# Gated linear recurrence and an ELU network on one core: unit 0 first, weights between its steps, other DMA queues, decays a round ahead

## The chip, the core and the metric

The kernel runs on one core of a Trainium2 chip. The core has a matrix engine (TensorE, PE), a vector engine (VectorE, DVE), an activation engine (ScalarE, ACT), a general engine (GpSimd, POOL) and an engine that only issues transfers (SyncE, SP). Each engine takes its own queue of instructions in order, and semaphores hold an instruction until what it reads is there. The metric is the time of one execution on the device in microseconds; lower is better.

## The reference

```python
def _attn_ref(q, k, v, a_re, a_im):          # B, H, S, D = 4, 8, 768, 48
    mag = np.sqrt(a_re * a_re + a_im * a_im)
    scale = np.minimum(mag, 0.999) / (mag + 1e-06)
    a_re_n, a_im_n = (a_re * scale, a_im * scale)
    for t in range(S):
        ar, ai = (a_re_n[:, :, t, :, None], a_im_n[:, :, t, :, None])
        new_re = ar * S_re - ai * S_im
        new_im = ar * S_im + ai * S_re
        kv = np.einsum('bhd,bhe->bhde', k[:, :, t], v[:, :, t])
        S_re, S_im = (new_re + kv, new_im)
        y[:, :, t] = np.einsum('bhd,bhde->bhe', q[:, :, t], S_re)

def _moe_ref(x, w_in, w_out):                # x: 3072 x 384, w_in: 384 x 2048, w_out: 2048 x 384
    h = x @ w_in
    g = np.where(h > 0.0, h, np.exp(np.minimum(h, 0.0)) - 1.0)
    return (g @ w_out).astype(np.float32)
```

The output y of the first part, heads side by side, is x of the second. The two weights come as float64 and the kernel rounds them to float32 itself, from their two 32-bit words.

## The kernel before

The 3072 tokens are cut into 12 units of 256: 128 positions of a pair of the four sequences. A unit goes through three groups of stages.

The decays (`squares`, `logarithms`, `angles`, `carried`) turn a_re and a_im into a logarithm l and an angle th. The gating (`turns`, `decays`, `waves`, `gated`) sums them along the positions on TensorE, takes exponentials E and F and cosines and sines cs, and multiplies them into q and k, which gives qg and kg. E's rows at the end of each 64 positions also go out to memory (`ends`) and come back transposed as T. The recurrence, for each of the two sequences n, transposes qg and kg (`transposed`), forms scores and masks them (`scores`, tile a), carries the state S over two blocks of 64 positions (`states`; S = (S + kv) * T on VectorE and GpSimd) and sums the output y (`values`). `seam` then copies y by DMA into x, in which 384 features lie over three groups of 128 partitions.

The network follows: `hidden` makes two of the 16 blocks of g (six products, then Relu and Exp on ScalarE and one fused step on VectorE), eight calls to a unit; `project` makes a quarter of the 16 products of one 128-token half, eight calls to a unit. The PSUM tiles of `hidden` and `project` share three buffers (tag mlp), those of the other products share three more (tag w).

The order is written out by hand. A step has 16 slots; in each slot stand the recurrence of unit step - 2, the gating of unit step - 1, the decays of unit step, one weight piece while there are any, and one call of `hidden` or `project` for unit step - 3 (lists CC, BB, A and M). So unit 0 crosses three steps before its first `hidden`, and the 28 weight pieces (12 of w_in, 512 columns, and 16 of w_out, 128 rows) stand one to a slot in the first 28 slots. `load_weights` loads a piece and rounds it with six steps on VectorE and one addition on GpSimd between them. All transfers but carry (the phase that one unit hands to the unit after next) are issued by SyncE.

Of the kernel before, what the change touches and what calls it, by code (L numbers as in the profile page):

```python
# [29 lines left out]
WC = 512  # L30
# [22 lines left out]
def _general(  # L53
# [291 lines left out]
    def seam(y_sb):  # L345
        x = sb.tile([C, NI, GT], FP32, tag="x", bufs=2, name="x")
        for h in range(H):
            e = 0
            while e < D:
                i, r = divmod(h * D + e, C)  # L350
                n = min(D - e, C - r)
                nc.sync.dma_start(
                    out=x[ds(r, n), i], in_=y_sb[ds(h % 2 * HP + e, n), h // 2]
                )
                e += n
        return x
# [81 lines left out]
def kernel(  # L438
# [87 lines left out]
    def load_weights(dst, src):  # L526
# [3 lines left out]
        if src.dtype == FP32:  # L530
            nc.sync.dma_start(out=dst, in_=src)
            return
        n = dst.shape[-1]
        w = sb.tile([C, n, 2], U32, tag="g", bufs=5, name="w64")
        nc.sync.dma_start(out=w.rearrange("p n two -> p (n two)"), in_=src)
        lo, hi = w[:, :, 0], w[:, :, 1]
        f = sb.tile([C, n], U32, tag="ee", bufs=4, name="wf")
        p = sb.tile([C, n], U32, tag="ee", bufs=4, name="wp")
        nc.vector.tensor_scalar(
# [3 lines left out]
        nc.vector.scalar_tensor_tensor(  # L543
            out=f, in0=hi, scalar=TOP, in1=p, op0=ALU.bitwise_and, op1=ALU.bitwise_or
        )
        nc.vector.tensor_scalar(
# [3 lines left out]
        nc.vector.scalar_tensor_tensor(  # L550
            out=p, in0=lo, scalar=2.0**-52, in1=p, op0=ALU.mult, op1=ALU.mult
        )
        nc.gpsimd.tensor_tensor(out=p, in0=p, in1=f, op=ALU.add)  # L553
        nc.vector.tensor_scalar(
            out=hi, in0=hi, scalar1=EXP, scalar2=None, op0=ALU.bitwise_and
        )
        nc.vector.scalar_tensor_tensor(
# [6 lines left out]

    def new(tag, bufs=1, shape=None):
        return sb.tile(shape or [C, NB, H, D], FP32, tag=tag, bufs=bufs, name=tag)

    def squares(u):
        x = nat[u]
        ar, ai = x["ar"], x["ai"]  # L570
        nc.vector.tensor_reduce(
# [6 lines left out]
        x["m2"], sq = new("m2"), new("e")  # L578
        nc.scalar.activation(out=x["m2"], in_=ar, func=AF.Square)
        nc.scalar.activation(out=sq, in_=ai, func=AF.Square)  # L580
        nc.gpsimd.tensor_tensor(out=x["m2"], in0=x["m2"], in1=sq, op=ALU.add)  # L581

    def logarithms(u):


        x = nat[u]
        ar, ai = x["ar"], x["ai"]
        lm, lr = x["m2"], new("lr")
        nc.scalar.activation(out=lm, in_=lm, func=AF.Ln)
        nc.scalar.activation(out=lr, in_=ar, func=AF.Ln)  # L590
        e, x0 = new("e"), new("x0")
        nc.scalar.activation(out=x0, in_=lr, func=AF.Exp, scale=-1.0)
        nc.scalar.activation(out=e, in_=lm, func=AF.Exp, scale=-0.5, bias=ln_eps)  # L593
        nc.gpsimd.tensor_tensor(out=lr, in0=ar, in1=x0, op=ALU.mult)
        nc.gpsimd.tensor_tensor(out=x0, in0=ai, in1=x0, op=ALU.mult)
        x["l"] = new("l")
        nc.vector.scalar_tensor_tensor(  # L597
            out=flat(x["l"]), in0=flat(lm), scalar=2 * float(np.log(CAP)), in1=flat(e),
            op0=ALU.min, op1=ALU.subtract,
        )  # L600
        nc.vector.scalar_tensor_tensor(
            out=flat(x0), in0=flat(lr), scalar=-2.0, in1=flat(x0), op0=ALU.add, op1=ALU.mult
        )
        x["t"] = x0
# [3 lines left out]
    def angles(u):  # L608
        x = nat[u]
        x["th"] = new("th")  # L610
# [12 lines left out]
    def turns(u):  # L623
        x = nat[u]
        x["z"] = new("z")
        for n in range(NB):
# [5 lines left out]
            r = new("rnd", 2, [C, HD])  # L632
# [11 lines left out]
    def decays(u):  # L644
        x = nat[u]
        x["E"], x["F"] = new("E"), new("F")
        x["T"] = new("T", 3, [2 * D, NB, C // L, H])
# [12 lines left out]
        nc.sync.dma_start(  # L660
# [3 lines left out]
        for i in range(2):  # L664
            for n in range(NB):
# [83 lines left out]
    def values(u, n):  # L749
# [17 lines left out]
        if n == 0:  # L767
            x["y"] = new("y", 1, [C, NP, GT])
# [167 lines left out]
```

## Time and profile before

| | us |
|---|---|
| median of three runs | 917.97 (916.97 to 921.32) |
| the profiled execution | 920.53 |
| its span, first to last instruction | 918.7 |
| TensorE busy in it | 716.1 |
| ScalarE, VectorE, GpSimd busy | 369.8, 301.9, 227.0 |

The profile's groups name a line, an engine, an operation, and the tile that is written and those that are read; behind them stand the busy time, the mean duration in ns, the idle time ahead of the group and what ended it. A matrix product in float32 is two instructions in these counts. Windows give, for a stretch of the span, its length and then the busy time of TensorE, its weight loads, VectorE, ScalarE and GpSimd, TensorE's granted clock (1.00 is full), the share of the DMA engines and GB/s.

### The profile page before, as it was taken

The numbers are of one execution on the slowest core, as the hardware profiler recorded it, in microseconds if no ns is written. First come the engines' busy times: TensorE is split into PE (matmuls) and PEld (weight loads), VectorE is DVE, ScalarE is ACT, GpSimd is POOL, SyncE is SP. The second block draws the span as 40 slices with busy tenths as digits, with TensorE's granted clock in tenths as the row PEclk, the third lists the DMA queues.
The fourth block names the chain that finished last, engine by engine and source line by source line (L and its number), as shares of the span: only waits on it lengthen the run. The fifth ranks groups of instructions, "written<-read, shape, count | busy, mean of one in ns | idle before, by whom it ended". The sixth has DMA issues, their size and how long they took to land.

```text
span 918.7 us, 13005 instructions
## 1 busy us (share of the span) xinstructions
PE 716.1 (78%) x5346; PEld 523.7 (57%) x5346; DVE 301.9 (33%) x454; ACT 369.8 (40%) x555; POOL 227.0 (25%) x159
## 2 busy tenths in 40 slices
PE   0100002749999999899999999999999999999997
PEld 0000002538667677576676676776766767778684
DVE  2777875314233232133142331331422312112020
ACT  2310302617437257165273381562733714433040
POOL 1322425222302312313233123132330230110000
PEclk9955556659999999999999999999999999999999
DMA  8243143230142212311411422124113021010100
GB/s 210 60 169 103 20 136 68 37 69 3 34 86 37 48 40 37 76 12 35 87 20 22 83 36 56 33 35 86 25 23 76 3 54 33 2 35 2 35 2 20
DMA packets 177485, 47.04 MB, mean 51 GB/s; under 512 B 165720, under 2 KB 173832, under 8 KB 177416
## 3 DMA queue, kind: packets, MB, share of 16 engines
q1 hardware_dynamic: 177096, 46.09, 24.7%
q8 instruction: 44, 0.72, 0.3%
q14 instruction: 25, 0.20, 0.1%
q0 software_dynamic: 320, 0.03, 0.0%
HBM read 36.55 MB, written 4.79 MB: 45 GB/s over the span
## 4 chain that ended last, share of the span: by engine, by line
PE 48%; POOL 14%; issue 12%; SPq 10%; DVE 10%; DMA 4%; ACT 1%; POOLq 0%; DVEq 0%
PE mlp L797 25%; PE mlp L813 12%; SPq L783 5%; POOL kg L689 4%; SPq L509 3%; POOL wp L553 3%; PE w L704 2%; PE w L712 2%; POOL F L686 2%; POOL E L686 2%; PE w L733 2%; DMA x<-y 2%; DVE wf L543 2%; DVE wp L550 2%; PE y L762 1%
## 5 line engine op out<-in xcount | busy, mean ns | idle before, releaser
L797 PE MATMUL mlp<-x,w_in 128*128 128x256 f32 x1152 | 277.9, 392 | 30.1 <-DMA x<-y 23.6
L797 PEld LDWEIGHTS mlp<-x,w_in 128*128 128x128 f32 x1152 | 218.3, 195 | 73.7 <-issue 18.7
L813 PE MATMUL mlp<-w_out,g 128*128 128x384 f32 x768 | 258.5, 490 | 0.0
L813 PEld LDWEIGHTS mlp<-w_out,g 128*128 128x128 f32 x768 | 143.2, 190 | 92.7
L804 DVE SCALAR_TENSOR_TENSOR g<-ee,mlp 128x512 f32<-128x512 f32 x96 | 64.3, 685 | 271.6 <-ACT ee L803 271.6
L802 ACT ACTIVATE ee<-mlp 128x512 f32<-128x512 f32 x96 | 56.9, 593 | 150.9 <-PE mlp L797 149.1
L704 PE MATMUL w<-ident,qg 128*96 128x128 f32 x192 | 27.2, 288 | 107.6 <-DVE qg L689 107.6
L745 POOL TENSOR_TENSOR S<-S,T 96x384 f32<-96x384 f32 x40 | 33.0, 825 | 273.2 <-DVE S L744 252.4
L819 ACT COPY o<-mlp 128x384 f32<-128x384 f32 x24 | 11.5, 479 | 213.8 <-PE mlp L813 213.8
L704 PEld LDWEIGHTS w<-ident,qg 128*96 128x96 f32 x192 | 21.9, 132 | 112.7 <-DVE qg L689 99.2
L581 POOL TENSOR_TENSOR m<-m,e 128x768 f32<-128x768 f32 x12 | 21.7, 1812 | 175.7 <-ACT e L580 175.7
L803 ACT ACTIVATE ee<-ee 128x512 f32<-128x512 f32 x96 | 60.5, 630 | 2.8
L553 POOL TENSOR_TENSOR wp<-wp,wf 128x384 f32<-128x384 f32 (+1 forms) x28 | 32.1, 1145 | 100.5 <-DVE wp L550 97.6
L628 PE MATMUL w<-th,sum_turns 128*128 128x384 f32 x48 | 19.6, 534 | 43.3 <-ACT th L611 43.3
L689 DVE TENSOR_TENSOR qg<-E,cs 128x1536 f32<-128x1536 f32 x12 | 21.1, 1758 | 93.0 <-POOL E L686 93.0
L733 PEld LDWEIGHTS w<-vn,kg 64*96 64x96 f32 x704 | 37.3, 172 | 17.7 <-issue 9.6
L733 PE MATMUL w<-vn,kg 64*96 64x48 f32 x704 | 40.5, 257 | 7.6 <-DVE z L636 7.6
L597 DVE SCALAR_TENSOR_TENSOR l<-m,e 128x768 f32<-128x768 f32 x12 | 23.6, 1968 | 66.1 <-ACT e L593 66.1
L705 ACT COPY qt<-w 96x512 f32<-96x512 f32 x48 | 25.8, 584 | 40.7 <-PE w L704 40.7
L689 POOL TENSOR_TENSOR kg<-F,cs 128x1536 f32<-128x1536 f32 x12 | 41.6, 3463 | 0.9
L744 DVE TENSOR_TENSOR S<-w,S 96x384 f32<-96x384 f32 x40 | 22.1, 552 | 51.1 <-PE w L733 35.6
L628 PEld LDWEIGHTS w<-th,sum_turns 128*128 128x128 f32 x48 | 9.9, 210 | 47.7 <-ACT th L611 43.3
(65 smaller groups left out, 730.8 us busy)
## 6 DMA issues: line engine op xcount, KB each, us to landing
w<-in_moe_w_in_dram SPq DMA_DIRECT2D x12, 512.0 KB
w<-in_moe_w_out_dram SPq DMA_DIRECT2D x16, 384.0 KB
ar<-in_a_re_dram SPq DMA_DIRECT2D x24, 192.0 KB
ai<-in_a_im_dram SPq DMA_DIRECT2D x24, 192.0 KB
q<-in_q_dram SPq DMA_DIRECT2D x24, 192.0 KB
k<-in_k_dram SPq DMA_DIRECT2D x24, 192.0 KB
vn<-in_v_dram SPq DMA_DIRECT2D x24, 192.0 KB
out_dram<-o SPq DMA_DIRECT2D x24, 192.0 KB
```

What stands on the lines that cost most here:

```text
L553: nc.gpsimd.tensor_tensor(out=p, in0=p, in1=f, op=ALU.add)
L686: nc.gpsimd.tensor_tensor(out=g, in0=x[key], in1=g, op=ALU.mult)
L689: eng.tensor_tensor(out=o, in0=g.rearrange("p n h d -> p (n h) d").unsqueeze(2).to_broadcast(shape), in1=x["cs"], op=ALU.mult,)
L704: nc.tensor.transpose(t[:, h], x[key + "g"][:, n, h0 + h], ident)
L733: nc.tensor.matmul(g[:, h], lhsT=x["kg"][ts(c, L), n, h], rhs=vn[u % 2][ts(c, L), n, h, 0:D], start=True, stop=True,)
L745: nc.gpsimd.tensor_tensor(out=new_s, in0=new_s, in1=wide, op=ALU.mult)
L783: nc.sync.dma_start(out=x[ds(r, n), i], in_=y[ds(h % 2 * HP + e, n), h // 2])
L797: nc.tensor.matmul(t[:, e], lhsT=w_in[:, i, ts(f + e, C)], rhs=x["x"][:, i], start=(i == 0), stop=(i == NI - 1),)
L802: nc.scalar.activation(out=e, in_=t, func=AF.Relu, scale=-1.0)
L803: nc.scalar.activation(out=e, in_=e, func=AF.Exp, scale=-1.0)
L804: nc.vector.scalar_tensor_tensor(out=x["g", f // 4][:, f % 4 : f % 4 + 2], in0=e, scalar=-1.0, in1=t, op0=ALU.add, op1=ALU.max)
L813: nc.tensor.matmul(x["o"], lhsT=x["g", f // 4][:, f % 4, ts(n, C)], rhs=w_out[:, f], start=(f == 0), stop=(f == NF - 1),)
```

## The change

**Order.** Unit 0 goes straight through all its stages before anything else, with steps of the weight rounding between them. Then come rounds of 16 slots. Round r holds `hidden` of unit r, the gating and the recurrence of unit r + 1, and `project` of units r - 1 and r - 2 (four calls each; of unit 0 all eight in round 1 and the next slot). Units 1 and 2 have their decays in the same round as their gating. From unit 3 on the decays stand a round ahead, in slots 8 to 12.

**Weights.** They are cut into 14 parts (6 of w_in, 1024 columns; 8 of w_out, 256 rows). A part's seven steps are all on VectorE and are handed out one by one: 22 in unit 0, 56 in round 0, the rest in the first slots of round 1. The rows of w_in are loaded in an order of their own: the 48 + 16 + 48 + 16 rows of each group of 128 partitions are chosen so that `values` can write three quarters of x straight from PSUM in place, and `seam` moves only 16-partition pieces, six instead of ten.

**Queues.** `seam` and T go by GpSimd's queue, `ends` by ScalarE's. T is two transfers of 48 x 32 single elements instead of four of half that size.

**Engines and buffers.** The products of `squares`, `logarithms` and the k side of `gated` are on VectorE for unit 0, and on GpSimd later; q's two products are on VectorE always. Most tiles of the decays and the gating share one tag with six buffers; kg, kt and o have one buffer instead of two.

On TensorE, at the start of the program, this stood before (qg, kg, qt and kt are the gated q and k and their transposes, vn is v, sum_turns and sum_logs are constant matrices):

```order
L628 MATMUL w<-th,sum_turns 128x384 x2
L650 MATMUL w<-l,sum_logs 128x384 x2
L704 MATMUL w<-ident,qg 96x128 x8
L704 MATMUL w<-ident,kg 96x128 x8
L628 MATMUL w<-th,sum_turns 128x384 x2
L712 MATMUL w<-qt,kt 64x64 x16
L733 MATMUL w<-vn_72,kg 96x48 x16
L650 MATMUL w<-l,sum_logs 128x384 x2
```

And this stands at the end of unit 0's recurrence now, with unit 1 behind it (the tag n holds th and l):

```order
L790 MATMUL y<-a,vn_72 64x64 x16
L797 MATMUL y<-qt,S 48x64 x8
L831 MATMUL mlp<-x,w_in 128x256 x24
L664 MATMUL w<-n,sum_turns 128x384 x2
L686 MATMUL w<-n,sum_logs 128x384 x2
L739 MATMUL w<-ident,qg 96x128 x8
L831 MATMUL mlp<-x,w_in 128x256 x6
```

The sums of the next unit, which stood among unit 0's products, now stand behind unit 0's first four `hidden` calls.

On VectorE, in round 0, the rows around unit 1's rounding are now these (L838 is g, L567 to L585 are the weight steps, L669 and L672 the rounding of the summed angle):

```order
L621 SCALAR_TENSOR_TENSOR n<-n 128x768
L626 SCALAR_TENSOR_TENSOR n<-n 128x768
L634 TENSOR_REDUCE least<-ar 128x1
L637 TENSOR_REDUCE most<-ai 128x1
L838 SCALAR_TENSOR_TENSOR g<-ee,mlp 128x512
L567 TENSOR_SCALAR wp<-w_427 128x1024
L571 SCALAR_TENSOR_TENSOR wf<-w_427,wp 128x1024
L574 TENSOR_SCALAR wp<-wf 128x1024
L838 SCALAR_TENSOR_TENSOR g<-ee,mlp 128x512
L578 SCALAR_TENSOR_TENSOR wp<-w_427,wp 128x1024
```

Before, a piece's steps stood together, and the decays and the rounding between whole pieces; now single steps alternate with the stages.

On VectorE, in a steady round, the rows from the second block's state on were these before:

```order
L744 TENSOR_TENSOR S_3459<-w,S_2610 96x384
L744 TENSOR_TENSOR S_3462<-w,S_3459 96x384
L597 SCALAR_TENSOR_TENSOR l<-m_3370,e 128x768
L601 SCALAR_TENSOR_TENSOR x_3486<-lr,x_3486 128x768
L804 SCALAR_TENSOR_TENSOR g<-ee,mlp 128x512 x4
L717 TENSOR_TENSOR a<-w,mask 128x512
```

and are these now:

```order
L779 TENSOR_TENSOR S<-w,S 96x384 x2
L621 SCALAR_TENSOR_TENSOR n<-n 128x768
L626 SCALAR_TENSOR_TENSOR n<-n 128x768
L634 TENSOR_REDUCE least<-ar 128x1
L637 TENSOR_REDUCE most<-ai 128x1
L838 SCALAR_TENSOR_TENSOR g<-ee,mlp 128x512 x3
L752 TENSOR_TENSOR a<-w,mask 128x512
```

The two fused steps of the decays have changed places, and the two reductions stand behind them, ahead of the last three g of the unit that is in `hidden`.

The core of the diff:

```diff
-        nc.gpsimd.tensor_tensor(out=p, in0=p, in1=f, op=ALU.add)
+        yield nc.vector.tensor_tensor(out=p, in0=p, in1=f, op=ALU.add)
...
+    def products(u):
+        return nc.vector if u == 0 else nc.gpsimd
...
-        nc.sync.dma_start(
+        nc.scalar.dma_start(
             out=ends.rearrange("n c h d -> c n (h d)"),
             in_=x["E"][L - 1 :: L].rearrange("p n h d -> p n (h d)"),
         )
-        for i in range(2):
-            for n in range(NB):
-                nc.sync.dma_start(
-                    out=x["T"][ts(i, D), n].rearrange("p c h -> p (c h)"),
-                    in_=ends[n].rearrange("c h d -> d (c h)"),
-                )
...
+        for i in range(2):
+            nc.gpsimd.dma_start(
+                out=x["T"][ts(i, D)].rearrange("p n c h -> p (n c h)"),
+                in_=x["ends"].rearrange("n c h d -> d (n c h)"),
+            )
...
+        for j in range(2):
+            for i in range(NI):
+                nc.gpsimd.dma_start(
+                    out=x["x"][ds(j * HP + D, G), i], in_=x["y"][ds(j * HP + i * G, G)]
                 )
...
+    once = recurrence(decaying(0, 1, 1, 3, 3) + gating(4, 5, 5, 6), 7)
+    steady = recurrence(gating(0, 1, 2, 3), 6)
+    early = decaying(8, 9, 9, 12, 12)
...
+    between = {angles: 3, decays: 4, gated: 4}
+    for at, fn in once:
+        fn(0)
+        if fn is gated:
+            load_qk(1)
+        converts(between.get(fn, int(at >= 7)))
+    load_v(1)
+    for at, fns in enumerate(plan):
+        if at < 2 * SLOTS:
+            fetches(1 if at < 8 else at % 2)
+            converts(3 if at < 8 else 4 if at < SLOTS else 3)
+        for fn in fns:
+            fn()
```

`recurrence(first, base)` lays the transposes, scores, states and values of the two sequences at slots base + 0 to base + 8 and `seam` at base + 9; `converts(n)` issues the next n steps of the weight rounding.

More of the change, by code (lines that the diff above doesn't have):

```diff
@@ new lines, with fetches, converts @@
+    parts = [("in", m) for m in range(NI * DF // WC)] + [("out", m) for m in range(NF // WF)]
+    ahead, steps = list(parts), []
+    def fetches(n):
+        for kind, m in ahead[:n]:
+            fetch(kind, m)
+        del ahead[:n]
+    def converts(n):
+        for _ in range(n):
+            while not steps or next(steps[0], None) is None:
+                del steps[:1]
+                if not parts:
+                    return
+                steps.append(rounded(*parts.pop(0)))
+    SLOTS = 16
@@ new lines, in recurrence @@
+    def recurrence(first, base, n_only=None):
+        at = [[0, 1, 2, 3, 5], [3, 4, 6, 7, 8]]
+        fns = [
+            [
+                lambda u, n=n: transposed(u, "q", n), lambda u, n=n: transposed(u, "k", n),
+                lambda u, n=n: scores(u, n), lambda u, n=n: states(u, n),
+                lambda u, n=n: values(u, n),
+            ]
+            for n in range(NB)
+        ]
+        plan = [(base + x, fn) for n in range(NB) for x, fn in zip(at[n], fns[n])]
+        return sorted(first + plan + [(base + 9, seam)], key=lambda x: x[0])
```

264 lines of the change are left out of this document (134 added, 130 removed).

## The prediction

> **What bounds the kernel now.** I read the page from the top, then cut the span where the first product of the second half, `hidden`, begins.
>
> ```profile
> span 918.7 us, 13005 instructions
> PE 716.1 (78%) x5346; PEld 523.7 (57%) x5346; DVE 301.9 (33%) x454; ACT 369.8 (40%) x555; POOL 227.0 (25%) x159
> PE   0100002749999999899999999999999999999997
> ```
> ```profile
> 0.00:197.30 197.30, 30.08 (x280) 22.43 (x280) 115.73 (x197) 47.46 (x59) 66.97 (x55) 0.66 0.41 98
> 197.30:324.70 127.40, 121.29 (x883) 87.77 (x883) 35.69 (x48) 60.55 (x92) 32.10 (x20) 0.95 0.25 44
> 324.70:758.60 433.90, 412.43 (x3193) 300.82 (x3193) 124.33 (x168) 212.18 (x322) 117.61 (x76) 0.98 0.25 44
> 758.60:912.30 153.70, 152.29 (x992) 112.66 (x992) 26.13 (x41) 49.19 (x82) 10.32 (x8) 1.00 0.08 18
> 912.30:918.70 6.40, 0.00 (x0) 0.00 (x0) 0.00 (x0) 0.46 (x1) 0.00 (x0) 0.84 0.10 36
> ```
>
> TensorE (first column after the length) is full from 197 us on and nearly idle before: of the 202.6 us it idles, 167 lie ahead of 197.3, 29 in the three rows between, 6.4 behind its last product. The view of waits says for whom it waits:
>
> ```profile
> PE w L704 <- DVE qg L689: 107.6, 2, 98.5
> PE w L628 <- ACT th L611: 43.3, 1, 43.3
> PE mlp L797 <- DMA x<-y: 23.6, 21, 3.1
> ACT z L676 <- DMA carry<-z: 1.3, 1, 1.3
> ```
>
> The first 147 us are VectorE's: it runs 28 weight conversions in a row while unit 0 waits between them for its step. In the steady part a unit waits once, for x to land. So there are two questions: when does a full TensorE begin, and what does each later round wait for? TensorE's products themselves are the same in both kernels.
>
> **The opening: what VectorE carries.**
>
> ```profile
> L539 DVE TENSOR_SCALAR wp<-w 128x512 uint32<-128x512 uint32 x12 | 5.0, 420 | 16.4 <-DMA w<-in_moe_w_in_dram 16.3
> L539 DVE TENSOR_SCALAR wp<-w 128x384 uint32<-128x384 uint32 x16 | 5.6, 352 | 2.2 <-DMA w<-in_moe_w_out_dram 2.1
> L543 DVE SCALAR_TENSOR_TENSOR wf<-w,wp 128x512 uint32<-128x512 uint32 x12 | 8.3, 693 | 0.4
> L543 DVE SCALAR_TENSOR_TENSOR wf<-w,wp 128x384 uint32<-128x384 uint32 x16 | 8.9, 559 | 0.6
> L553 POOL TENSOR_TENSOR wp<-wp,wf 128x512 f32<-128x512 f32 x12 | 16.0, 1333 | 54.2 <-DVE wp L550 54.2
> ```
>
> 128 columns more cost 0.068 us in the first kind and 0.134 in the second. Carried on (an estimate) a 1024-wide step takes 0.69 or 1.23 us, a 768-wide one 0.56 or 0.96. A part is three steps of the first kind, three of the second and the addition. The addition has no VectorE row at this width; I take the second kind (below it lies the first kind, above it POOL's 1.33 per 512). That is 7.0 us for each of 6 w_in parts and 5.5 for each of 8 w_out parts, 86 us in all. What matters is where they stand, since VectorE takes its queue in order. The other durations:
>
> ```profile
> 4.92 1.28 ACT L579 ACT_TABLE_LOAD   x1 [4.92 <-DMA ar<-in_a_re_dram]
> L589 ACT ACTIVATE m<-m 128x768 f32<-128x768 f32 x12 | 10.1, 843 | 58.9 <-POOL m L581 58.8
> L655 ACT ACTIVATE E<-w 128x384 f32<-128x384 f32 x24 | 11.8, 492 | 26.7 <-PE w L650 26.7
> L705 ACT COPY qt<-w 96x512 f32<-96x512 f32 x48 | 25.8, 584 | 40.7 <-PE w L704 40.7
> L594 POOL TENSOR_TENSOR lr<-ar,x 128x768 f32<-128x768 f32 x12 | 21.8, 1816 | 49.2 <-DMA T<-ends 36.7 <-ACT x L592 12.5
> L595 POOL TENSOR_TENSOR x<-ai,x 128x768 f32<-128x768 f32 x12 | 28.2, 2353 | 0.9
> L686 POOL TENSOR_TENSOR F<-k,F 128x768 f32<-128x768 f32 x12 | 21.6, 1803 | 0.0
> L689 POOL TENSOR_TENSOR kg<-F,cs 128x1536 f32<-128x1536 f32 x12 | 41.6, 3463 | 0.9
> L689 DVE TENSOR_TENSOR qg<-E,cs 128x1536 f32<-128x1536 f32 x12 | 21.1, 1758 | 93.0 <-POOL E L686 93.0
> L601 DVE SCALAR_TENSOR_TENSOR x<-lr,x 128x768 f32<-128x768 f32 x12 | 11.5, 956 | 17.1 <-POOL x L595 17.1
> L571 DVE TENSOR_REDUCE least<-ar 128x1 f32<-128x768 f32 x12 | 11.3, 944 | 0.0
> L636 DVE TENSOR_TENSOR z<-w,rnd 128x384 f32<-128x384 f32 x24 | 13.4, 557 | 0.8
> L804 DVE SCALAR_TENSOR_TENSOR g<-ee,mlp 128x512 f32<-128x512 f32 x96 | 64.3, 685 | 271.6 <-ACT ee L803 271.6
> L803 ACT ACTIVATE ee<-ee 128x512 f32<-128x512 f32 x96 | 60.5, 630 | 2.8
> ```
>
> Unit 0, from 4.92: table load and two squares to 7.9; the addition, half of qg's 1.76, on VectorE to 8.8; Ln, Ln, load, Exp, Exp to 13.8; two products, two fused steps and two reductions on VectorE to 18.5; three conversion steps to 21.2; four rounding steps to 23.5; three Sin/Abs steps (their load is hidden) to 26.1; load and four half-width Exp to 29.2; four gating products on VectorE, 5.3, to 34.5. The recurrence then has TensorE to itself, at a low clock and with a copy between steps: about 21 us for its 16 us of products, to 55.5.
>
> ```profile
> L642 POOL DMA_DIRECT2D carry<-z x10 | 5.6, 560 | 26.6 <-DVE z L636 23.6 <-DVE wp L539 3.0
> DMA to landing us min/median/max: 1.6/1.6/3.5
> 629.55 6.23 SPq L783 DMA_DIRECT2D x<-y  x10
> ```
>
> The seam is two PSUM copies (0.9), six issues on POOL at carry's 0.56, and carry's 1.6 to land: 5.9. So the first `hidden` starts at **61.5** instead of 197.3. The old seam's ten issues took 6.2 on SP.
>
> Unit 1 follows its whole chain inside round 0. Its four first `hidden` calls end at 74. Squares, Ln and Exp stand in ACT's queue behind the first Relu/Exp pair and end at 72.8; POOL's two products end at 76.1, and VectorE stands still from 70.7 until then. Behind that wait are queued two fused steps, two reductions, three g and nine conversion steps, 15 us, ahead of unit 1's rounding: z at 93.3. Sin, load, Exp take it to 99. The gating on VectorE and POOL reads two SBUF tensors on both and partly takes turns: qg at 103.5, kg near 107. From there VectorE alone sets the pace: 31 conversion steps and its g, a and S are 35 us, so the second `values` starts at about 139.5 and x lands, 1.7 + 5.9 later, at **147**. Hiding: the conversions' loads run two parts ahead; without that each costs its landing.
>
> Unit 2 again runs its chain within round 1: squares at 142, POOL's products at 155, rounding at 171 behind one g and eight conversion steps, gating at 181. TensorE has six `hidden` until 165 and waits 13 us. After that it owes 12 us of recurrence, two `hidden` and seven `project`, 2.6 each: round 2 begins at **218**.
>
> **The steady rounds.**
>
> ```profile
> 574.20:635.20 61.00, 57.72 (x456) 42.07 (x454) 17.76 (x24) 30.31 (x46) 16.87 (x11) 1.00 0.26 46
> 579.00 2.76 PE L797 MATMUL mlp<-x,w_in 128*128 128x256 f32 x12
> 581.59 1.45 PE L628 MATMUL w<-th,sum_turns 128*128 128x384 f32 x4
> 912.28 0.48 ACT L819 COPY o<-mlp 128x384 f32<-128x384 f32 x1 [9.84 <-PE mlp L813]
> ```
>
> A round of today takes 61.0 us, 57.7 of it products; a `hidden` or `project` call is 2.6 (start to start), so 16 of them and 16.1 of recurrence. In the new order four `project` calls stand between the seam and the first `hidden`: x's six issues lie behind 10 us of products, and that wait goes. What is late next is slot 12. A `project` there takes the PSUM buffer of the sixth `hidden`, so it needs that call's g; the g stands in VectorE's queue behind the early decays of the next unit. Counted from the start of slot 8: Relu/Exp 1.2, two squares 1.7, again 1.2, two copies 1.1, load and two Ln 2.9, load and Exp 2.1, with a wait for products of 1.5: the first Exp ends at 11.7. Then POOL's two products to 15.9, two fused steps and two reductions to 19.7, g to 20.3. TensorE is there after 18.0, so it waits **2.3** a round. ACT's one further table load a unit (Arctan and Sin no longer stand together) and VectorE's 2.7 of gating lie under the 57.7, in queues that are half empty by the row above.
>
> **Sum.** Round 2 has three `project` calls less and a gating chain that ends late (57.7 - 7.8 + 4.1 = 54); rounds 3 to 9 take 7 x 60.0 = 420; round 10, without early decays, 57.7; the 28 calls left 72.8; the tail 6.4 (912.3 to 918.7). 218 + 54 + 420 + 57.7 + 72.8 + 6.4 = 829 of span. The profiled execution took 920.53, 1.8 over its span, and the median, 917.97, is 2.6 below it: 829 + 1.8 - 2.6 = 828, say **829 us**. Nearly all of the 90 us comes out of the opening.
>
> **Unknown costs.** T's gather moves from SP to POOL as two transfers of 1536 single elements (48 x 32), and no POOL transfer of that kind is in the trace:
>
> ```profile
> q0 software_dynamic: 320, 0.03, 0.0%
> ```
> ```profile
> 105.22 0.67 POOL L642 DMA_DIRECT2D carry<-z  x1 [3.01 <-DVE wp L539]
> ```
>
> Carry's ten transfers made 320 packets, 32 each, in 0.56 us. If the issue alone counts, T costs 0.56; if every element costs as much as one of those packets (0.0175), 27 us. Below zero it cannot go, since SP's T was waited for by nobody on the path. I take 2 us, near the low end, since carry's is the only row of that queue; two T of unit 0 are then landed at 38, ahead of S at 43. The other cost is POOL's issues beside VectorE's conversions: between nothing and one 0.69 step for each of some 24 issues of the first three units, 17 us; I take nothing, since the one carry that was issued among conversions, at 105.22, took 0.67 against 0.56. Steady waits may lie between 0 and twice 2.3: 20 us either way over nine rounds.
>
> Here rules of the Trainium skill speak against the change. "SBUF — State Buffer", section "SBUF: two separate sides", holds that POOL writes descriptors itself and is locked out while VectorE runs a two-port operation; it gives 620 ns alone and 3100 beside a copy. The one row here of that sort, carry at 105.22, shows 0.11 us. By its figures, an estimate, the eight issues of each of the first three units would cost up to 60 us more; my 17 goes by the longest step.
>
> **Rivals.** *POOL's element-wise T becomes the bound* (the slower side). In a steady round kg ends at 17 and the next squares' addition is due at 28, so two T fit while one takes up to 5.6 us. Beyond, each microsecond of one T delays decays and S by 2 us in each of 8 rounds and in the three opening units: 22 us. The 91 us are gone at 9.7 us a T, 6 ns an element; at 12 it gives 970, at 27 over 1250. For it: the spread of the two ends; against: the one wait for a POOL transfer today is 1.3 us in ten carries. Chance 9%. *The opening is VectorE's longer than I count* (locks against POOL, loads of w_out that come one conversion late, a T of 6 us): 850 to 895. Chance 17%. *The steady wait is not there and VectorE's queue drains earlier* (for it: the addition on VectorE and the 1024-wide steps are estimates; TensorE at 57.7 a round): 829 - 18 - 25 = 785. Chance 15%. *The opening gains nothing because TensorE's order brings unit 0 no earlier to x*: 910 to 920, chance 2%; the order of the first rows speaks against it. My forecast, 805 to 850, has 57%.
>
> **Range and signs.** The forecast and its two neighbours make up 89%; 785 to 895 holds about 85 in 100, and the far end of T stays outside. A measurement of this kernel tells about 0.5% (4.6 us) from no change: faster 0.89, within 0.02, slower 0.09.
>
> **What will show it.** First `hidden` near 61, unit 1's x near 147, round 2 near 218; VectorE busy nearly throughout 60 to 145; a wait of `project` for g of 2 to 3 us a round, and none of `hidden` for x; POOL's T rows near 1 to 2 us. Wrong if T takes over 6 us, if TensorE stands before the transposes in the steady rounds, or if unit 0's x comes after 80.

## The result, and the profile after

The changed kernel takes **858.3 us** (median of four runs, 857.1 to 860.4) against 917.5 of the kernel before on the same chip: a ratio of 0.936, with a 95% interval of 0.931 to 0.940. The prediction was 829, with a range of 785 to 895. So 59 of the 88 us that were forecast are there, and this part is about the 29 that are not.

The page of the changed kernel, first its span, then busy time, then the 40 slices of TensorE and the clock granted to it in tenths:

```profile
span 858.6 us, 12795 instructions
PE 721.1 (84%) x5346; PEld 529.8 (62%) x5346; DVE 327.6 (38%) x401; ACT 388.2 (45%) x591; POOL 235.3 (27%) x210
PE   1436283559978998999999999999999989999997
PEclk9667586778989999999999999999999999999999
```

TensorE now idles 137.5 us (858.6 - 721.1) instead of 202.6: 65 us less. But it is busy 5 us longer than before (721.1 against 716.1) with the same products, so some of them ran slower. The view of waits says for whom it idles:

```profile
PE w L739 <- DVE qg L719: 36.5, 4, 11.4
PE mlp L831 <- DMA x<-y: 23.2, 2, 15.3
PE w L664 <- ACT n L647: 21.0, 2, 16.7
PE mlp L847 <- DVE g L838: 16.9, 8, 2.2
```

The waits of `hidden` for x are two, both in the opening, where there were 21; the new one is of `project` for g, eight times 2.1 us. To find the 29 us, the marks of the prediction are looked up in TensorE's timeline (start, length, what ended the idle time before): the first `hidden` of units 0 and 1, the `turns` with which rounds 2, 3 and 10 begin, and the last products.

```profile
66.96 13.46 PE L831 MATMUL mlp<-x,w_in 128*128 128x256 f32 x48 [15.35 <-DMA x<-y]
153.28 10.15 PE L831 MATMUL mlp<-x,w_in 128*128 128x256 f32 x36 [7.85 <-DMA x<-y]
232.74 1.45 PE L664 MATMUL w<-n,sum_turns 128*128 128x384 f32 x4
292.39 1.45 PE L664 MATMUL w<-n,sum_turns 128*128 128x384 f32 x4
722.41 1.45 PE L664 MATMUL w<-n,sum_turns 128*128 128x384 f32 x4
823.59 28.65 PE L847 MATMUL mlp<-w_out,g 128*128 128x384 f32 x88
```

| from, to | predicted | measured | off |
|---|---|---|---|
| start to the first `hidden` | 61.5 | 67.0 | +5.5 |
| to unit 1's first `hidden` | 85.5 | 86.3 | +0.8 |
| to round 2 | 71 | 79.5 | +8.5 |
| round 2 | 54 | 59.7 | +5.7 |
| rounds 3 to 9 | 420 | 430.0 | +10.0 |
| round 10 and the last 28 calls | 130.5 | 129.8 | -0.7 |
| tail | 6.4 | 6.4 | 0 |

Three places carry it: the first landing of x, rounds 1 and 2, and 1.4 us in each steady round.

**A steady round.** In the windows of after (length, then busy time of TensorE, its weight loads, VectorE, ScalarE, GpSimd, then the granted clock, DMA share and GB/s) round 2, round 4 and the stretch behind round 9 read:

```profile
232.74:292.39 59.65, 52.26 (x434) 39.84 (x432) 19.34 (x25) 31.51 (x48) 22.38 (x21) 0.94 0.23 41
353.95:415.52 61.57, 58.99 (x457) 43.37 (x456) 19.57 (x25) 31.89 (x49) 21.07 (x18) 0.97 0.23 42
722.41:852.24 129.83, 129.82 (x683) 91.03 (x681) 20.21 (x30) 34.93 (x60) 13.59 (x13) 1.00 0.04 13
```

A round is 61.57 instead of 60.0, TensorE is busy 58.99 in it instead of 57.7, and the clock is 0.97. Cut finer at the wait, TensorE's timeline and then the windows show where:

```profile
399.86 4.54 PE L847 MATMUL mlp<-w_out,g 128*128 128x384 f32 x8 [2.10 <-DVE g L838]
405.82 2.85 PE L847 MATMUL mlp<-w_out,g 128*128 128x384 f32 x8
```
```profile
398.00:399.90 1.90, 0.04 (x1) 0.04 (x1) 1.90 (x4) 0.00 (x0) 0.00 (x0) 1.00 0.11 21
399.90:403.30 3.40, 3.40 (x6) 1.87 (x7) 1.80 (x3) 3.34 (x4) 0.00 (x0) 0.51 1.23 211
403.30:406.00 2.70, 2.70 (x37) 1.97 (x36) 1.02 (x2) 0.02 (x1) 0.00 (x0) 0.98 0.09 11
```

The wait is 2.1 us, as forecast (2.3). What was not forecast stands behind it: for 3.4 us TensorE is granted half its clock, and the `project` call that took 2.85 elsewhere takes 4.54. **The wait costs 2.1, and another 1.7 after it.** What it waits for is in VectorE's timeline:

```profile
395.66 0.96 DVE L621 SCALAR_TENSOR_TENSOR n<-n 128x768 f32<-128x768 f32 x1 [8.69 <-POOL n L620]
396.54 0.95 DVE L626 SCALAR_TENSOR_TENSOR n<-n 128x768 f32<-128x768 f32 x1
397.41 0.95 DVE L634 TENSOR_REDUCE least<-ar 128x1 f32<-128x768 f32 x1
398.27 0.94 DVE L637 TENSOR_REDUCE most<-ai 128x1 f32<-128x768 f32 x1
399.13 1.28 DVE L838 SCALAR_TENSOR_TENSOR g<-ee,mlp 128x512 f32<-128x512 f32 x2
```

### The profile page after: what moved, and what is told of

It is laid out like the page before. It is cut to its first block, busy times and chain, and to the rows that moved or that the text cites. A ratio compares the mean times of both kernels' runs of the same rounds, so it can differ in the third digit from the quotient of the medians.

```text
span 858.6 us, 12795 instructions
## 1 busy us (share of the span) xinstructions
PE 721.1 (84%) x5346; PEld 529.8 (62%) x5346; DVE 327.6 (38%) x401; ACT 388.2 (45%) x591; POOL 235.3 (27%) x210
## 4 chain that ended last, share of the span: by engine, by line
PE 58%; issue 16%; DVE 10%; POOL 8%; ACT 4%; DMA 2%; SPq 1%; DVEq 0%; POOLq 0%; ACTq 0%
PE mlp L847 29%; PE mlp L831 18%; PE w L739 3%; PE w L768 2%; POOL n L619 2%; POOL n L620 2%; DMA w<-in_moe_w_in_dram 2%; PE y L797 2%; PE w L747 2%; PE w L664 1%; DVE g L838 1%; DVE least L634 1%; POOL S L780 1%; DVE most L637 1%; PE w L686 1%
## 5 line engine op out<-in xcount | busy, mean ns | idle before, releaser
L831 PE MATMUL mlp<-x,w_in 128*128 128x256 f32 x1152 | 273.8, 392 | 23.3 <-DMA x<-y 23.2
L847 PE MATMUL mlp<-w_out,g 128*128 128x384 f32 x768 | 271.3, 507 | 16.9 <-DVE g L838 16.9
L838 DVE SCALAR_TENSOR_TENSOR g<-ee,mlp 128x512 f32<-128x512 f32 x96 | 65.0, 685 | 214.6 <-ACT ee L837 211.7
L853 ACT COPY o<-mlp 128x384 f32<-128x384 f32 x24 | 11.5, 479 | 130.5 <-PE mlp L847 124.5
L719 POOL TENSOR_TENSOR kg<-k,cs 128x1536 f32<-128x1536 f32 x11 | 51.9, 4718 | 0.9
L805 ACT COPY x<-y 128x384 f32<-128x384 f32 x24 | 11.3, 473 | 89.5 <-PE y L797 89.5
L621 DVE SCALAR_TENSOR_TENSOR n<-n 128x768 f32<-128x768 f32 x12 | 11.5, 958 | 91.4 <-POOL n L620 91.4
L664 PE MATMUL w<-n,sum_turns 128*128 128x384 f32 x48 | 21.8, 586 | 27.0 <-ACT n L647 21.0
L717 POOL TENSOR_TENSOR k<-k,n 128x768 f32<-128x768 f32 x11 | 23.9, 2171 | 71.7 <-ACT n L691 71.7
L819 POOL DMA_DIRECT2D x<-y x72 | 35.5, 500 | 26.7 <-ACT y L809 26.7
L669 DVE TENSOR_SCALAR rnd<-w 128x384 f32<-128x384 f32 x24 | 13.4, 557 | 73.7 <-PE w L664 72.4
L606 POOL TENSOR_TENSOR n<-n 128x768 f32<-128x768 f32 x11 | 19.9, 1810 | 77.9 <-ACT n L605 77.9
L768 PEld LDWEIGHTS w<-vn,kg 64*96 64x96 f32 x704 | 34.5, 161 | 9.5 <-issue 9.3
L619 POOL TENSOR_TENSOR n<-ar,n 128x768 f32<-128x768 f32 x11 | 20.1, 1824 | 63.8 <-ACT n L617 63.8
```

The lines of the kernel that those rows point to most:

```text
L619: products(u).tensor_tensor(out=lr, in0=ar, in1=x0, op=ALU.mult)
L664: nc.tensor.matmul(t, lhsT=sum_turns, rhs=x["th"][:, n].rearrange("p h d -> p (h d)"), start=True, stop=True,)
L719: eng.tensor_tensor(out=o, in0=g.rearrange("p n h d -> p (n h) d").unsqueeze(2).to_broadcast(shape), in1=x["cs"], op=ALU.mult,)
L768: nc.tensor.matmul(g[:, h], lhsT=x["kg"][ts(c, L), n, h], rhs=vn[u % 2][ts(c, L), n, h, 0:D], start=True, stop=True,)
L819: nc.gpsimd.dma_start(out=x["x"][ds(j * HP + D, G), i], in_=x["y"][ds(j * HP + i * G, G)])
L831: nc.tensor.matmul(t[:, e], lhsT=w_in[:, i, ts(f + e, C)], rhs=x["x"][:, i], start=(i == 0), stop=(i == NI - 1),)
```

## Experiments

All ratios are to the kernel before, run beside them. The lines of kernels with added code are shifted by a few.

### The wait for g, and the half clock behind it

**Reductions later.**

```diff
-    early = decaying(8, 9, 9, 12, 12)
+    early = decaying(8, 9, 12, 12, 12)
```

> Computes the same; only the two reductions of the early decays stand at slot 12 instead of 9. Theory: in each steady round project waits 2.1 us for the sixth g, which stands behind two fused steps and two reductions in VectorE's queue, and after that wait TensorE is granted 0.50 for about 3.4 us, another 1.7 us. Without the reductions (1.8 us) the wait is 0.3 to 0.5, as long as the waits of 0.47 elsewhere in the round after which the clock stays at 1.00: rounds of 58.1 instead of 61.5, eight of them, 858.3 - 27 = 831. Rival 1, the half clock comes from something else that happens there (the loads of a that the reductions release): the wait goes, the half clock stays at slot 12 or moves with the loads to slots 12 to 13: 858.3 - 14 = 845. Rival 2, another wait takes its place (Relu/Exp behind Ln/Exp on ScalarE): 855 to 860.

Measured: 831.8 us, ratio 0.908 (0.905 to 0.911). The eight waits sum to 3.1 us, 0.4 at most, and the clock stays at 1.00, through the loads of a as well. The theory's number came out; the rivals are off by 13 us and more.

**Fused steps later too.** `logarithms` is cut in two, so that its steps on VectorE (`fused`) have a slot of their own; the six numbers are now the slots of `squares`, `logarithms`, `fused`, `noted`, `angles` and `carried`.

```diff
-    early = decaying(8, 9, 9, 12, 12)
+    early = decaying(8, 9, 12, 14, 12, 12)
```

> Computes the same; the two fused steps stand at slot 12 and the two reductions at slot 14, so nothing of the early decays stands between the last g of hidden. Theory: no wait of project for g is left and the granted clock stays at 1.00 through the round: 57.7 a round, 8 x 3.8 = 30 us less, 828. Against the run with the reductions alone moved it is 3 us faster (0.4 us of wait in each of eight rounds). Rival 1 (half clock has another cause): 841 to 845. Rival 2, what is moved is late for its own readers (a of slot 12 behind the fused steps, Arctan later): a wait of 1 to 3 us before values, 835 to 858.

Measured: 830.2 us, ratio 0.905 (0.902 to 0.908); no wait for g is left. That is 28.1 us less than the changed kernel, for one line of a slot table and a cut function. Its lead over the run before, 1.6 us where 3 were expected, lies inside the intervals and is not shown.

**One reduction later.** How long must a wait be? Only the second reduction moves, to slot 12 (the fourth number).

```diff
+    early = decaying(8, 9, 9, 12, 12, 12)
```

> Computes the same; the changed kernel with only the second of the two reductions of the early decays moved to slot 12, so that the wait of project for g in each steady round is 2.1 - 0.87 = 1.25 us, between the waits of 0.47 that left the clock at 1.00 and those of 2.1 that were followed by half clock. Theory A, a wait of 1.25 us is enough: 0.50 for about 3.4 us after it, 2.95 us a round lost, 858.3 - 8 x 0.87 = 851. Theory B, it is not: 1.25 us a round lost, 858.3 - 8 x 2.55 = 838, and the granted clock stays at 1.00 in slots 12 and 13.

Measured: 838.6 us, ratio 0.912 (0.910 to 0.915), theory B. The call behind the wait is at full speed:

```profile
394.89 2.85 PE L849 MATMUL mlp<-w_out,g 128*128 128x384 f32 x8 [1.25 <-DVE g L840]
```

So 1.25 us were not followed by half clock in any of eight rounds. But length is not all of it. In the changed kernel the first wait, in round 2, goes free and the next one doesn't:

```profile
278.42 2.85 PE L847 MATMUL mlp<-w_out,g 128*128 128x384 f32 x8 [2.08 <-DVE g L838]
338.29 4.54 PE L847 MATMUL mlp<-w_out,g 128*128 128x384 f32 x8 [2.10 <-DVE g L838]
```

**More work in a round.** That called for a test of *when* a wait falls.

```diff
+    def more(u):
+        t = work([C, HD])
+        for n in (320, 320, 300):
+            nc.tensor.matmul(
+                t[:, 0:n], lhsT=ident, rhs=w_in[:, 0, 0:n], start=True, stop=True
+            )
...
+        if 3 <= u <= 9:
+            put(u * SLOTS + 4, more, u)
```

> Computes the same and more: in rounds 3 to 9 three matrix products whose results nobody reads (1.58 us) stand ahead of the first hidden. In the changed kernel the waits of 2.1 us at slot 12 were followed by half clock in rounds 3 to 9 and not in round 2; from round 2's wait to round 3's pass 59.85 us, from there on 61.57. Theory: activity is judged in windows of about 3.41 us (as long as the half clock lasts) that run by themselves; 61.57 is 18.04 windows, 59.85 is 17.53, so round 2's wait falls across a border and the later ones within one window. With 1.58 us more a round takes 61.44, 18.00 windows, so the waits of rounds 3 to 9 stay where round 2's fell, no half clock follows, and the 7 x 1.58 = 11.1 us of added work cost 7 x 1.7 = 11.9 less: 857.5, rounds of 61.44 at a granted clock of 1.00. Rival 1: every such wait in a steady round is followed by half clock: 858.3 + 11.1 = 869.4. Rival 2: the phase drifts and half clock comes back in some of the rounds: 859 to 868.

Measured: 855.4 us (853.7 to 859.2), ratio 0.930 (0.927 to 0.932): **11 us of added products, and the kernel is no slower.** All eight waits, still 2.1 us, go free; the second and a whole round:

```profile
338.94 2.85 PE L854 MATMUL mlp<-w_out,g 128*128 128x384 f32 x8 [2.11 <-DVE g L838]
```
```profile
365.81:427.27 61.46, 58.88 (x464) 43.70 (x463) 19.50 (x25) 31.87 (x49) 21.07 (x19) 1.00 0.22 41
```

Rival 1 is out by 14 us, and rival 2 by the clock, which is 1.00 behind each wait. One rival was not named: the added products might keep the clock up by themselves. The trace of the changed kernel, which has none, speaks against it. Cut into windows there, these are the two parts of round 2's wait, and the half clock of rounds 3 and 7:

```profile
276.34:277.09 0.75, 0.00 (x0) 0.00 (x0) 0.75 (x2) 0.00 (x0) 0.00 (x0) 1.00 0.00 0
277.09:278.42 1.33, 0.00 (x0) 0.00 (x0) 1.33 (x3) 0.00 (x0) 0.00 (x0) 1.00 0.22 39
338.53:341.94 3.41, 3.41 (x6) 1.75 (x6) 1.76 (x4) 3.15 (x4) 0.00 (x0) 0.50 1.20 204
584.29:587.70 3.41, 3.23 (x5) 1.85 (x6) 2.02 (x4) 3.13 (x4) 0.00 (x0) 0.50 1.19 208
```

From 338.53 to 584.29 pass 245.76 us, 72 times 3.413, while four rounds of waits take 246.18: the half clock keeps a time of its own, and in round 7 it begins 0.18 us before the wait ends. All changes of the clock in this trace, and in those of the other runs, lie on such a grid, each trace with its own start. In round 2 an instant of it, 277.09, cuts the wait into 0.75 and 1.33 us; in rounds 3 to 9 at least 1.89 us of each wait lie between two instants. With the added products the larger part of a wait is 1.45 at most. In the run with one reduction later, five of the eight waits of 1.25 lie whole between two instants.

So TensorE's activity is judged in windows of about 3.41 us that run by themselves, and a wait of 2.1 us costs 2.1 or 3.8 according to where it falls: up to 1.45 us of waiting in one window went free in these runs, and 1.89 did not. The Trainium skill, "TensorE: Matmul & The Clock Gate", section "What's actually happening", has such free-running windows of 3413 ns, and this agrees. Its section "HAM oscillation — how this bites in real kernels" sets the limit for idle gaps at about 3.4 us; here gaps of 2.1 us were enough in seven of eight rounds, and the measurement decides.

### The first x lands late

In the changed kernel unit 0's recurrence ends 4 us earlier than forecast, and x's six transfers are issued by 55.8. They land at 66.9. SP's timeline, POOL's, and the times to landing of the tile x:

```profile
50.14 8.17 SPq L555 DMA_DIRECT2D w<-in_moe_w_in_dram  x8
```
```profile
52.59 3.17 POOL L819 DMA_DIRECT2D x<-y  x6 [1.15 <-ACT y L809]
```
```profile
DMA to landing us min/median/max: 1.6/1.6/13.5
```

**Bulk held back.** SP first stores 16 elements of x to a scratch tensor, and so waits for it, before it issues the last w_in transfers.

```diff
+    landed = dram.tile([G, 1], FP32, tag="landed", bufs=1, name="landed")
+    nc.sync.dma_start(out=landed, in_=nat[0]["x"][ds(HP + D, G), NI - 1, 0:1])
     for at, fns in enumerate(plan):
```

> Computes the same, and writes 16 elements of unit 0's x to a scratch tensor: SP does not issue the last eight w_in transfers (and what stands behind them) before unit 0's x has landed. Theory: x's six transfers are issued on POOL's queue by 55.8 and land only at 66.9, because the 2 MB of w_in issued from 50.1 on stand in the same DMA engines; held back, x lands 1.6 to 2 us after its last issue, the first hidden starts at 57.5 instead of 66.96, VectorE's 15.3 us of idling become about 6, and the w_in parts 5 and 6 still come before their conversion: 9 us less, 849. Rival 1: POOL's own queue is slow there (locked out by VectorE's conversion steps, or slow in writing its descriptors): the first hidden stays at 65 to 67 and the time at 858. Rival 2: the first hidden comes early, but round 0 goes by VectorE's conversions or by their later loads: 853 to 858.

Measured: 849.7 us, ratio 0.926 (0.924 to 0.929), as the theory has it (849); `hidden` starts at 56, with the transfers still on POOL's queue:

```profile
55.97 12.73 PE L831 MATMUL mlp<-x,w_in 128*128 128x256 f32 x48 [4.65 <-DMA x<-y]
```

**The seam back on SP.**

```diff
-                nc.gpsimd.dma_start(
+                nc.sync.dma_start(
                     out=x["x"][ds(j * HP + D, G), i], in_=x["y"][ds(j * HP + i * G, G)]
```

> Computes the same; the seam's six transfers go back to SP's queue, and that part of the change (small transfers on other queues than the bulk) is undone for x. Theory: a queue of its own does not protect a small transfer, the order of issue does: on SP the six stand ahead of the last w_in transfers, x lands near 57.5 and the first hidden starts there: about 849, like the run that holds the bulk back. In the steady rounds SP has nothing that waits at the time of the seam (loads of a at 398, out at 416, the seam at 411 in round 5), and ten us of project stand between seam and hidden: nothing changes there. Rival 1: SP is behind other waits (out, loads of a) in the steady rounds and x comes late: a wait of hidden for x of 2 to 20 us a round, slower than 858. Rival 2: on SP x lands late for the bulk that is already under way (k, v of unit 1): the first hidden at 60 to 66, 852 to 858.

Measured: 854.5 us, ratio 0.932 (0.928 to 0.935), between theory and no change. The time lies in rival 2's range, but not for its reason, a first `hidden` at 60 to 66. Unit 0 is early, by the order of issue, but unit 1 pays, which neither the theory nor the rivals had: its y is copied by 134.4, and on SP its x then stands behind two w_out parts whose issue takes 10.6 us. TensorE's timeline, and SP's:

```profile
57.05 12.08 PE L831 MATMUL mlp<-x,w_in 128*128 128x256 f32 x48 [4.51 <-DMA x<-y]
151.52 10.04 PE L831 MATMUL mlp<-x,w_in 128*128 128x256 f32 x36 [17.84 <-DMA x<-y]
```
```profile
136.05 10.61 SPq L555 DMA_DIRECT2D w<-in_moe_w_out_dram  x2
146.72 3.69 SPq L819 DMA_DIRECT2D x<-y  x6
```

So a queue of its own saves the small transfer from standing behind the issue of bulk (unit 1: 10 us), and not from bulk that is already issued (unit 0: 10 us). The Trainium skill, "DMA: Bandwidth & Descriptors", section "Issuing engines are not separate DMA queues", says the second: all run on the same 16 DMA engines. The trace agrees.

**Both edits**, the fused steps and reductions late and the bulk held back:

> Computes the same; fused steps and reductions behind the last g, and the last w_in transfers held back until unit 0's x has landed. Theory: the two causes lie in different parts of the span and add: 830.2 - 8.6 = 821.6, between 819 and 824, with the first hidden near 56 and steady rounds of 57.7. Rival: the opening's gain is lost where round 1 and 2 wait for gating: 826 to 830.

Measured: 820.6 us, ratio 0.895 (0.893 to 0.897). The two add: 28.1 + 8.6 = 36.7, and 37.7 are seen.

### Round 1: gating beside conversions

Unit 2's chain runs inside round 1 and TensorE waits 11.1 us for its qg. In VectorE's and POOL's timelines of the changed kernel a conversion step that takes 0.55 elsewhere stood ahead of it for 3.72. It began 0.12 us after POOL's product and ended 0.4 us after it:

```profile
186.31 3.72 DVE L582 TENSOR_SCALAR w<-w 128x768 uint32<-128x768 uint32 x1
```
```profile
186.19 3.43 POOL L719 TENSOR_TENSOR kg<-k,cs 128x1536 f32<-128x1536 f32 x1
```

**Conversions out of the way**, on top of both edits:

```diff
-            converts(3 if at < 8 else 4 if at < SLOTS else 3)
+            converts(3 if at < 8 else 4 if at < SLOTS else 3 if at < 19 else 0 if at < 23 else 6)
```

> Computes the same; the run with both edits, and no conversion step in slots 3 to 6 of round 1: eleven steps of w_out move to slots 7 and 8, where VectorE idles. Theory: in round 1 TensorE waits 11.1 us for unit 2's qg, and 4 to 5 us of it are two conversion steps and a g in VectorE's queue ahead of q and qg, one of them 3.72 us long instead of 0.55 since POOL multiplies k at that time; without them q starts where E and F end: 4.5 us less, 817. Rival 1: g, which stays ahead of q, waits for ScalarE as long, and q and qg share the port with POOL's k and kg (3.24 instead of 1.76): 1 to 2 us less, 820. Rival 2: project waits for the last w_out parts: 822 to 826.

Measured: 816.3 us, ratio 0.891 (0.889 to 0.893): 4.2 us less, the sum that was expected, by half another way. The wait for unit 2's qg fell by 1.5 only, from 11.1 to 9.7; the one before its `turns` fell from 6.2 to 4.3. For the lock has only moved: now q itself stood beside kg.

```profile
171.85 4.12 DVE L722 TENSOR_TENSOR q<-q,n 128x768 f32<-128x768 f32 x1
```

**Gating on VectorE alone** for units 1 to 3, q first for all units, and one slot earlier in units 1 and 2:

```diff
-        for key, by in (("k", "F"), ("q", "E")):
-            eng = products(u) if key == "k" else nc.vector
+        for key, by in (("q", "E"), ("k", "F")):
+            eng = nc.gpsimd if key == "k" and u > 3 else nc.vector
...
-    once = recurrence(decaying(0, 1, 1, 1, 3, 3) + gating(4, 5, 5, 6), 7)
+    once = recurrence(decaying(0, 1, 1, 1, 3, 3) + gating(4, 5, 5, 5), 7)
```

> Computes the same; the run with all edits so far (fused steps and reductions late, bulk held back, no conversions in slots 3 to 6 of round 1), and units 1 to 3 multiply k and q on VectorE alone, q first, in units 1 and 2 one slot earlier and so ahead of two g. Theory: VectorE's q took 4.12 us in round 1 instead of 0.95 since it stood still until POOL's kg was done, and its qg 3.24 in rounds 0 and 2 instead of 1.76; without POOL's two products beside them qg of unit 2 is done at 172.5 instead of 177.8 and that of unit 3 1.5 us earlier; in round 0 the 2.7 us of k and kg that VectorE takes over cancel what it no longer waits: 816.3 - 5.3 - 1.5 = 809.5. Rival 1: the long q is VectorE's own (its operands, not POOL): 5.4 us of gating in a row, 815 to 820. Rival 2: the g that stand behind the gating now hold the PSUM buffers and hidden waits: 811 to 815.

Measured: 807.0 us, ratio 0.878 (0.873 to 0.883). The same two steps take 0.96 and 1.76 with POOL out of the way, and the wait for unit 2's qg falls from 9.7 to 4.1 (unit 1's is 7.5):

```profile
171.34 0.96 DVE L722 TENSOR_TENSOR q<-q,n 128x768 f32<-128x768 f32 x1 [5.72 <-ACT n L696]
172.34 1.76 DVE L724 TENSOR_TENSOR qg<-q,cs 128x1536 f32<-128x1536 f32 x1
```

Of the 9.3 us that this run gained (6.8 expected), some are the two g that stand behind the gating now; the run doesn't part them. The Trainium skill, "SBUF — State Buffer", section "Who interferes with whom", has the rule that fits: a VectorE step with two SBUF inputs and a GpSimd step that reads SBUF exclude each other for a whole instruction. The trace agrees for q, 4.12 against 0.96.

**Ln and Exp first** in round 0:

```diff
+    first = recurrence(decaying(0, 0, 1, 1, 2, 2) + gating(4, 5, 5, 5), 7)
...
-        for at, fn in once if u < 3 else steady:
+        for at, fn in first if u == 1 else once if u == 2 else steady:
```

> Computes the same; the run before, and unit 1's Ln and Exp stand in ScalarE's queue ahead of the first Relu/Exp pair of hidden, its Arctan one slot earlier. Theory: VectorE idles 6.1 us for the first g and 5.1 us for POOL's products of unit 1, since Ln and Exp stand behind the first pair although ScalarE idles 6.8 us ahead of it; in the new order Ln can start at 59 (POOL's addition stands behind the seam's issues) and the products end at 66.3 instead of 71.7, TensorE's wait of 4.3 us for Arctan goes, and VectorE, which sets the pace until unit 1's x, has 5 us less to idle: 809.5 - 5 = 804.5. Rival 1: the first pair is late by as much, hidden waits for its PSUM buffers and g: 808 to 812. Rival 2: VectorE's steps pace round 0 whatever comes first, the idling only moves: 809.

Measured: 802.9 us (800.7 to 806.3), ratio **0.875** (0.872 to 0.879), the lowest median here. Its interval overlaps that of the run before, so the 4.1 us between them are not shown by the times. The traces show that TensorE's wait of 4.3 for Arctan is 0.8 now, and that from unit 0's first `hidden` to unit 1's pass 81.1 us instead of 88.0.

### Parts of the change undone

**w_in parts in a row** ahead of unit 0's rounding:

```diff
-    between = {angles: 3, decays: 4, gated: 4}
+    between = {noted: 28}
...
-        converts(between.get(fn, int(at >= 7)))
+        converts(between.get(fn, 0))
```

> Computes the same; undoes one part of the change: four w_in parts (28 conversion steps) stand in one row on VectorE ahead of unit 0's rounding, and none between unit 0's later steps. Theory: 28 steps take 28 us, with a wait for the fourth part's load (issued at 35, 14 to land) until about 56, so unit 0's rounding comes at 58 instead of 23, its x near 90 without bulk beside it, and the first hidden starts near 91 instead of 67; when it starts VectorE has done as many steps as in the changed kernel (28 against 26), so nothing is won back: 858 + 24 = 882. Rival 1: round 0 is paced by what is left of VectorE's steps and its idling (15 us ahead of the first g) goes: 858 to 868. Rival 2: the loads that ran ahead free later waits and unit 1 gains: 870 to 878.

Measured: 877.2 us, ratio 0.957 (0.956 to 0.960), where the theory had 882. The steps between unit 0's stages are worth 18.9 us. The first `hidden` starts at 88.4, 21.4 later than in the changed kernel, and unit 1's at 170.0, 16.7 later: part of it is won back, which the theory denied and rival 2 had, and rival 1 is out.

**Decays in the same round** for all units:

```diff
-        for at, fn in once if u < 3 else steady:
+        for at, fn in once:
...
-        if u > 2:
+        if u > NU:
             for at, fn in early:
```

> Computes the same; undoes one part: all units prepare their decays in the round in which they are used (the order that units 1 and 2 have), none a round ahead. Theory: a steady round's decays take from its slot 0 two squares, addition, two loads, Ln, Exp, products, fused steps, Arctan and carried: 18 us, while TensorE has 10.6 us of project until turns at slot 4: a wait of 7.5 us; qg comes 14 us after turns and TensorE waits about 3 us for it, and each of the two waits is followed by half clock (1.7 us each); the wait for g at slot 12 (3.8) is gone. A round of 57.7 + 10.5 + 3.4 = 71.6 instead of 61.5, over eight rounds 80 us: 938. Rival 1: project and hidden hide the chain and only the wait for g goes: 828 to 845. Rival 2: the half clock comes once only, or the loads of a are late: 915 to 960.

Measured: 1019.1 us, ratio 1.113 (1.109 to 1.117), where 938 was expected. The sign was right and the size was not: twice what I counted. The view of waits and one row of VectorE's timeline:

```profile
PE w L739 <- DVE qg L719: 130.8, 12, 11.6
PE w L664 <- DVE n L653: 65.8, 10, 13.9
```
```profile
500.29 4.11 DVE L717 TENSOR_TENSOR q<-q,n 128x768 f32<-128x768 f32 x1
```

A round takes 78.5 us where 71.6 were expected. The wait for turns is 5.7 a round (7.5 expected), but that for qg is 11 instead of 3: from turns to qg pass 23 us, not 14, with table loads, Relu/Exp pairs and g in the queues and q locked out beside kg. Without decays a round ahead this order is slower than the kernel before.

## Why the prediction was right, and by what it was off

- **The opening as the source of the gain: right.** TensorE's idle time fell by 65 us, steady rounds hardly changed (62.0 on average before, 61.4 after). Unit 0's rounding ended at 23.3 (23.5 predicted) and its gating at 34.3 (34.5). From the first `hidden` to unit 1's the step held to 0.8 us, but this is luck in part: the second `values` began at 140.9, 74.0 us behind the first `hidden` where 78 were forecast, and x landed 12.4 us behind that where 7.5 were forecast. VectorE was to be busy nearly throughout from 60 to 145; it was busy 61.7 of these 85 us and stood still from 58.7 to 74.0, ahead of the first g.
- **The seam: the term "carry's 1.6 to land" was mis-sized.** It landed 9.6 us later than that (shown by holding the bulk back). The carry at 105.22 that gave the row was issued at a DMA share of 0.00 (104 to 110 us). The recurrence, 4 us shorter than I took it, hid part of it: +5.5.
- **The steady wait: right in place and length** (2.1 for 2.3), **mis-sized in price.** The prediction charged the wait alone. Half clock behind it costs 1.6 to 1.7 more in each of rounds 3 to 9, 11.1 us in all (430.0 less 7 x 59.85); 10.0 show, since a round without it takes 59.85, a little less than the 60.0 that I counted. The trace of before had it, in rows that I averaged away; behind its waits for x, which come in pairs, the same eight products took 3.75 or 1.97:

```profile
387.01 0.70 PE L797 MATMUL mlp<-x,w_in 128*128 128x256 f32 x2 [2.08 <-DMA x<-y]
388.84 3.75 PE L797 MATMUL mlp<-x,w_in 128*128 128x256 f32 x8 [1.13 <-DMA x<-y]
573.88 0.67 PE L797 MATMUL mlp<-x,w_in 128*128 128x256 f32 x2 [0.75 <-DMA x<-y]
576.33 1.97 PE L797 MATMUL mlp<-x,w_in 128*128 128x256 f32 x8 [1.77 <-DMA x<-y]
```

  Short waits in one window add up there: a pair of 0.36 and 1.31, at 262 and 264, was followed by half clock too. The round that I took as the steady one, with 57.72 of products, was one without it.
- **Round 1, +8.5:** the terms that the prediction names for it (18 us up to the wait, 13 of waiting, 12 of recurrence, nine calls of 2.6) add to 66.4 and not to the 71 that it puts down; by its mark for the gating, 181, the wait would be 16. Against that the waits of 17.1 (6.0 and 11.1) are 1.1 too long, and 7.3 us are half clock behind waits, which it left out: 2.1 in the three `hidden` calls behind the wait for x, and 1.45, 1.3, 0.9 and 1.5 in the two calls behind each of the others. The waits are in part what VectorE lost beside POOL; with conversions and POOL moved away, 13.5 us went out of the opening.
- **Round 2, +5.7:** its own wait at slot 12 (2.1) was left out of "57.7 - 7.8 + 4.1", qg came 0.7 later (4.83 for 4.1), and 2.6 of half clock followed that wait, in calls that take 1.04 and 2.76 at full clock; 0.3 are not assigned.

```profile
248.07 1.94 PE L739 MATMUL w<-ident,qg 128*96 128x128 f32 x8 [4.83 <-DVE qg L719]
249.81 4.43 PE L831 MATMUL mlp<-x,w_in 128*128 128x256 f32 x12
```

- **The unknown costs.** T on POOL took 0.94 to 1.05 us a transfer (2 taken), nobody waited for it, and that rival is out. POOL's 72 issues of the seam took 0.48 to 0.63, the twelve among VectorE's conversion steps as well, so the term of nothing for them was right, and the lock that the prediction quotes against them is not seen. VectorE's steps beside POOL's products did stand still. The prediction allowed for that within the gating ("partly takes turns"), and left it out for the conversion steps beside it, of which one took 3.72 and another 4.21 in the opening (0.55 and 0.96 elsewhere).
- **The rival "longer opening" (850 to 895)** has the measured time, and half of the miss, 14.7 us, does lie ahead of round 2. But the causes that it names are not those that decided: bulk in the DMA engines and locks beside POOL's products are akin to them, and half clock is not among them.

## What to carry to other kernels

A short wait of TensorE has two prices: its length, and a stretch at half clock behind it if too much of it falls into one window of the clock. Read the granted clock and the duration of the products right behind a wait before costing it, and look for the rows in which the same wait was free. In a queue that is taken in order, a step that nobody waits for soon (here two reductions) belongs behind those that somebody does; this was worth 26.5 us in one line. And a small transfer needs both: a queue that doesn't wait, and no bulk issued just ahead of it.

## What was not expected of the hardware

- After a TensorE wait of 2.1 us, 3.4 us at a granted clock of 0.50, if 1.89 us or more of it lie in one window of 3.413 us; none where the larger part was 1.45 or less, and none after the eight waits of 1.25. Two shorter waits in one window, 0.36 and 1.31, had it as well.
- A VectorE step in SBUF can stand still until GpSimd's product is done: 4.12 instead of 0.96 (q), 3.72 instead of 0.55 (a conversion step). The twelve transfers that GpSimd issued among such conversion steps took 0.48 to 0.63 each.
- Six transfers of 16 KB took up to 13.5 us to land behind 2 MB of bulk from another queue, 1.6 without it.
